# A fused gated-recurrence and SwiGLU kernel: roots by a product for every chunk, gates in turns, decays by products, fills moved, dates shifted by stage

## The chip, the cores and the metric

The kernel runs on one core of a Trainium2 chip. The metric is the device time of one execution in microseconds. A core has a matrix engine (PE, with its weight loads shown as PEld), a vector engine (DVE), an engine for functions of one operand (ACT), a general engine (POOL), and a queue engine (SP) which here only starts transfers. ACT and POOL can start transfers too. Each engine runs its own list of instructions in order and waits on semaphores.

## The reference

```
# gateloop: batch 4, heads 8, 768 steps, head dimension 48
mag = sqrt(a_re^2 + a_im^2);  scale = min(mag, 0.999) / (mag + 1e-6)
for t in range(768):                       # complex decay for each head and row d
    S_re, S_im = ar*S_re - ai*S_im + k_t v_t^T,  ar*S_im + ai*S_re
    y_t = q_t @ S_re
# feed-forward on x = y as (3072 tokens, 384)
xn  = x / sqrt(mean(x*x) + 1e-6) * rms_g
g   = xn @ w_gate;  val = xn @ w_val       # 384 -> 1536
out = (g * sigmoid(g) * val) @ w_out       # 1536 -> 384
```

All inputs are float32 save the weights, which arrive in 64 bits and are narrowed on the chip.

## The kernel before, in words

The 3072 tokens are cut into 24 chunks of 128 (6 for each batch). A unit is the piece for which gates are worked out: units 0 and 1 hold one chunk each, the other eleven two chunks each. A group is two chunks that go through the feed-forward part together; there are 12.

- `load_gates(u)` and `load_kq(u)` bring a_re, a_im, q and k of a unit, features on the partitions. `gates(u)` has four stages of names: "size" (magnitudes, and a running product of them, with ACT and DVE), "root" (a reciprocal root of that product), "turn" (arctan of the gate, a running sum of angles, sine and cosine), and "rot" (q and k times size and angle, into `rots`). Arctan and sine, and the roots, need different tables on ACT, and a load of a table stands between them. Six transfers for each chunk carry `rots` to `kqs`, heads apart, and six for each unit carry the last column of the sizes, `ends`, to `decays`.
- `attend(n)` takes one chunk: S = k^T q by small products (32 rows each) into banks 4 and 5, a causal mask that DVE copies into `ams`, then y from `ams`, `ves` (the values) and the state of the chunk before, and the new state by way of `kts` and a product with `vns`. Transposes for `kts` use banks 7 and 4. The "norm" stage squares y, sums over features with a product with `ones` into one column of bank 7, writes that as `ssv` (DVE), raises it to -1/2 (POOL, `rss`), and spreads the root over all partitions. For chunks in `SENT`, 4 to 21, two POOL transfers do that, by way of a row of `sqs` to `row`; for the others a product with `ident` writes it into bank 7. DVE multiplies it into `xT`.
- `narrow(i)` brings one of 12 pieces of the weights by POOL's queue into a place that is free in `wo` or `hT`, and ACT and three DVE instructions narrow it. Pieces 0 to 5 are w_gate and w_val in turns (1.5 MB each), 6 to 11 are w_out. POOL keeps at most two under way; piece 3 waits besides for a chunk's kq to land (`CLEAR`).
- `feed(g)` multiplies xT by w_gate and w_val (banks 0 to 3 in turns, ACT takes silu, DVE the product into `hT`), then by w_out; from group 2 on by a scheme with fewer products. 
- `look(i)` reads the weights again to check their range, off the main work.

No instruction is issued where it is written. `add` notes each operation with its engine, an estimated duration and what it reads and writes; `note` derives what it must wait for, from overlapping boxes in a tile. `dates` works back from due times, `schedule` plays all engines forward with those durations and picks on each engine, among the operations that are ready, the one due first, and `issue` then emits everything in that order from one line, L667 of the profile. So one change in an estimate or a due time may reorder every engine. The dictionary `shift` moves the due times of a stage; it is empty here. Where PE would idle in the first 62 us (as planned), `schedule` puts in products of `rots` with itself as fillers, whose result nobody reads.

```
    SENT = range(4, N - 2)
...
        if n in SENT:
            line = sq[0:1, 1]
            dma(line, rss[n % 2], "POOL", slow=SLOW)
            wide = row
            dma(wide, line.unsqueeze(1).to_broadcast([1, P, C]), "POOL", slow=SLOW)
        else:
            wide = ps[:, 0:C]
            mms([(wide, rss[n % 2].to_broadcast([P, P]), ident, True, True)], 0.28)
```

## Time and profile before

| what | value |
|---|---|
| time, median of 3 runs | 730.87 us (729.05 to 731.51) |
| profiled execution, its own time | 727.01 us |
| its span, first to last instruction | 725.3 us |
| mean granted clock of PE | 0.988 |
| first product of the feed-forward part | 57.33 us |
| end of the last product on PE | 719.44 us |
| loads of ACT's table | 67, 1283 ns each |
| decay transfers on SP | 78 |
| root transfers on POOL | 36 |
| fillers on PE | 64 records, two for each product |

A row of the page gives engine, operation, output and inputs, the shapes, the number of records, and then busy time, the mean time of one, and idle time of the engine ahead of it with what ended it. A product in float32 shows as two records. Ends of products are modelled, so rows overlap: what a product costs is read from one start to the next. All operations of the fast path come from one line, so they are told apart by tiles.

### The profile page before, as it was taken

What the parts mean: (1) busy time and instruction counts of PE and PEld (TensorE: products, weight loads), DVE (VectorE), ACT (ScalarE), POOL (GpSimd) and SP (SyncE); (2) the same over time, 40 slices, a digit from 0 to 9 for tenths busy, and PEclk for the clock granted to TensorE, in tenths of its full rate; (3) what the DMA queues carried; (4) which work ended last, traced back from release to release, by engine and by line L of the source; (5) the groups of instructions that cost most, each with busy time, mean ns of one, the idle gap of its engine ahead of it and who ended that gap; (6) DMA issues with size and microseconds to landing.
All of it is one profiled execution on the core that took longest, in us unless ns stands there. A gap on an engine that the chain in (4) does not pass through costs nothing.

```text
span 725.3 us, 16217 instructions
## 1 busy us (share of the span) xinstructions
PE 682.6 (94%) x6870; PEld 596.2 (82%) x6870; DVE 470.0 (65%) x740; ACT 332.3 (46%) x450; POOL 70.4 (10%) x116
## 2 busy tenths in 40 slices
PE   0579999999999999999999999999999999999996
PEld 0468867886889889889889889889889889889885
DVE  5969898888879878879774656658544333134121
ACT  7639858867385864845461633626310110010010
POOL 6123100001100001011011011011011011000000
PEclk9978999999999999999999999999999999999998
DMA  8696665655466464566533333334133132100000
GB/s 296 214 310 190 194 185 156 180 143 128 132 149 155 142 168 119 164 141 170 140 87 76 85 63 63 100 67 91 42 62 61 37 66 34 36 13 2 23 0 27
DMA packets 105728, 81.84 MB, mean 113 GB/s; under 512 B 43664, under 2 KB 96144, under 8 KB 105648
## 3 DMA queue, kind: packets, MB, share of 16 engines
q1 hardware_dynamic: 100432, 64.99, 32.9%
q0 software_dynamic: 4416, 15.35, 9.2%
q8 instruction: 56, 0.92, 0.5%
q10 hardware_dynamic: 800, 0.39, 0.2%
q14 instruction: 24, 0.20, 0.1%
HBM read 55.84 MB, written 4.72 MB: 83 GB/s over the span
## 4 chain that ended last, share of the span: by engine, by line
PE 83%; DVE 5%; DMA 4%; ACT 3%; SPq 2%; issue 1%; POOL 0%; DVEq 0%; ACTq 0%
PE bank L667 83%; DMA ve<-in_v_dram 2%; SPq L667 2%; ACT turns L667 1%; DVE rot L667 1%; DVE turns L667 1%; DMA wo<-in_w_gate_dram 1%; ACT t L667 1%; ACT L667 1%; DMA kq<-rot 1%; DVE hT L667 1%; DMA in<-in_a_re_dram 1%; DVE in L667 0%; DVE t L667 0%; DVE wo L667 0%
## 5 line engine op out<-in xcount | busy, mean ns | idle before, releaser
L667 PE MATMUL bank<-xT,wg 128*128 128x256 f32 x864 | 200.9, 383 | 0.9 <-DVE xT L667 0.9
L667 PE MATMUL bank<-xT,wv 128*128 128x256 f32 x864 | 201.2, 382 | 0.4 <-DVE xT L667 0.4
L667 PEld LDWEIGHTS bank<-xT,wg 128*128 128x128 f32 x864 | 162.2, 191 | 22.8 <-DVE xT L667 1.1
L667 PEld LDWEIGHTS bank<-xT,wv 128*128 128x128 f32 x864 | 161.3, 190 | 23.5 <-issue 1.6
L667 ACT ACTIVATE sg<-bank 128x512 f32<-128x512 f32 x72 | 43.0, 597 | 169.4 <-PE bank L667 168.8
L667 PE MATMUL bank<-wo,hT 128*128 128x192 f32 (+1 forms) x576 | 117.7, 356 | 0.6 <-DVE hT L667 0.6
L667 DVE TENSOR_TENSOR hT<-bank,sg 128x512 f32<-128x512 f32 x72 | 49.5, 688 | 100.1 <-PE bank L667 88.5
L667 PEld LDWEIGHTS bank<-wo,hT 128*128 128x128 f32 x576 | 95.7, 190 | 12.9 <-DVE hT L667 1.1
L667 ACT ACT_TABLE_LOAD x67 | 86.0, 1283 | 16.1 <-DVE rot L667 7.1
L667 POOL TENSOR_TENSOR rs<-ssv,mhalf 128x1 f32<-128x1 f32 x24 | 25.3, 1054 | 498.6 <-DVE ssv L667 468.2
L667 DVE TENSOR_TENSOR rot<-kin,turns 128x768 f32<-128x768 f32 x48 | 44.1, 952 | 3.8 <-DMA kq<-rot 3.4
L667 PE MATMUL bank<-sums,hT 128*128 128x192 f32 x240 | 44.2, 327 | 0.0
L667 ACT ACTIVATE kt<-bank 128x384 f32<-128x384 f32 x40 | 19.2, 486 | 51.9 <-PE bank L667 32.3
L667 ACT ACTIVATE turns<-in 128x768 f32<-128x768 f32 (+1 forms) x39 | 30.1, 791 | 26.5 <-DVE rot L667 14.2
L667 PE MATMUL bank<-am,ve 128*32 128x128 f32 x768 | 39.2, 281 | 0.9 <-DMA ve<-in_v_dram 0.9
L667 PEld LDWEIGHTS bank<-sums,hT 128*128 128x128 f32 x240 | 39.7, 190 | 0.1
L667 PEld LDWEIGHTS bank<-kq 96*32 96x32 f32 x1536 | 30.2, 110 | 10.9 <-issue 7.0
L667 DVE TENSOR_TENSOR hT<-hT 128x768 f32<-128x768 f32 x40 | 38.2, 956 | 0.6
L667 PE MATMUL bank<-kq 96*32 96x128 f32 (+3 forms) x1536 | 35.2, 235 | 3.0 <-DMA kq<-rot 2.9
L667 PE MATMUL bank<-rot 128*128 128x128 f32 x64 | 12.2, 352 | 24.8 <-DVE rot L667 24.8
L667 DVE COPY_PREDICATED am<-causal,bank 128x512 f32<-128x512 int32 x48 | 33.9, 724 | 1.6 <-PE bank L667 1.1
L667 ACT ACTIVATE t<-t 128x768 f32<-128x768 f32 (+1 forms) x39 | 30.9, 792 | 8.7 <-DVE t L667 8.2
(115 smaller groups left out, 741.9 us busy)
## 6 DMA issues: line engine op xcount, KB each, us to landing
kq<-rot SPq DMA_DIRECT2D x144, 128.0 KB, 3.0
kin<-in_q_dram SPq DMA_DIRECT2D x24, 192.0 KB, 3.3
kin<-in_k_dram SPq DMA_DIRECT2D x24, 192.0 KB, 3.4
wo<-in_w_gate_dram SPq DMA_DIRECT2D x6, 768.0 KB, 5.0
out_dram<-ot SPq DMA_DIRECT2D x24, 192.0 KB, 2.2
wo<-in_w_val_dram SPq DMA_DIRECT2D x6, 768.0 KB, 5.7
wo<-in_w_out_dram SPq DMA_DIRECT2D x6, 768.0 KB, 4.3
in<-in_a_re_dram SPq DMA_DIRECT2D x11, 384.0 KB, 6.1
```

The source lines that it names most:

```text
L667: fn(*args, **kw)
```

## The change

Seven things change at once.

- `SENT` is empty: the root of every chunk is spread by a product with `ident`.
- `gates` yields ahead of "turn", and units 0 and 1 run in turns, size and root of both ahead of turn and rot of both; arctan waits for the last two roots.
- `send_decays`: for units 0 and 1, decays come by three small products of `ends` with selection matrices (built by DVE at the start in `ots`) and a copy, in place of six transfers each.
- Fills: most go from POOL to DVE with early due times, am1 to ACT; the causal mask takes 5 selections in place of 8.
- Operations of one `group` (the v transfers of a chunk, the kq transfers of a unit) don't wait for one another.
- DVE and ACT are `patient`: the plan may leave them idle for up to 1.5 us for an operation that is due much earlier. Piece 3 of the weights waits for the kq of chunk 1 in place of chunk 0.
- `shift` gets a table of 58 entries by stage.

```diff
--- before.py
+++ after.py
@@ -470,6 +470,7 @@
     LAND = 2.0
     LANES = 8
     turn = 0.0
+    patient = ("ACT", "DVE")
     BEGIN = {"SP": 0.8, "ACT": 0.8, "POOL": 0.8}
     TABLES = {"silu": ("S",), "sin": ("S", "T"), "arctan": ("T",), "rsqrt": ("A",)}
 
@@ -512,16 +513,16 @@
         for x in self.seen.get(name, ()):
             o, w, q0, q1, l, h = x
             over = q0 < p1 and p0 < q1 and l < hi and lo < h
-            if over and (write or w) and o != op["i"]:
+            if over and (write or w) and o != op["i"] and (not op["group"] or self.ops[o]["group"] != op["group"]):
                 op["deps"].add(o)
-            if not (write and p0 <= q0 and q1 <= p1 and lo <= l and h <= hi):
+            if op["group"] or not (write and p0 <= q0 and q1 <= p1 and lo <= l and h <= hi):
                 kept.append(x)
         kept.append((op["i"], write, p0, p1, lo, hi))
         self.seen[name] = kept
 
-    def add(self, eng, calls, dur, reads=(), writes=(), table=None, land=None, due=None, after=(), behind=(), late=None, mode=None):
+    def add(self, eng, calls, dur, reads=(), writes=(), table=None, land=None, due=None, after=(), behind=(), late=None, mode=None, group=None):
         op = dict(i=len(self.ops), eng=eng, calls=calls, dur=dur, deps=set(), table=table, land=land,
-                  base=due, late=late, mode=mode, stage=self.stage, behind={o["i"] for o in behind})
+                  base=due, late=late, mode=mode, group=group, stage=self.stage, behind={o["i"] for o in behind})
         self.ops.append(op)
         op["deps"].update(o["i"] for o in after)
         for ap in reads:
@@ -624,6 +625,14 @@
                 if pick is None or key < pick[0]:
                     pick = (key, o)
             o = pick[1]
+            if eng in self.patient:
+                for x in waiting[eng]:
+                    if t < ready[x["i"]] < t + o["dur"] - 0.2 and x["due"] < o["due"] - 50.0 and ready[x["i"]] < t + 1.5:
+                        pick = None
+                        free[eng] = max(free[eng], min(ready[y["i"]] for y in waiting[eng] if t < ready[y["i"]]))
+                        break
+                if pick is None:
+                    continue
             waiting[eng].remove(o)
             dur = o["dur"]
             if o["table"] and table not in self.TABLES[o["table"]]:
@@ -633,7 +642,7 @@
             if eng == "PE" and o["mode"] != mode:
                 mode = o["mode"]
                 dur += 0.06
-            if eng == "PE" and self.warm and t < self.warm["until"]:
+            if eng == "PE" and self.warm and t < self.warm["until"] and all("end" in x for x in self.warm["after"]):
                 since = max([free["PE"]] + [x["end"] + self.SYNC for x in self.warm["after"] if not recent])
                 n = int((t - since - 0.3) / 0.43)
                 if n > 0:
@@ -866,21 +875,28 @@
                  (width, -(RE_MAX - RE_MIN) / 2), (mhalf, -0.5), (zeros, 0.0)):
         fill(t, x)
     LATE = 12.0
+    add("POOL", [(make_identity, (nc, ident), {})], 0.5, [], [ident], due=-150.0)
+    fill(causal, 1.0, late=LATE)
+    for x, base in [(causal[:, 0], 0)] + [(causal[b * BLK:(b + 1) * BLK, 1], -BLK * (3 - b)) for b in range(4)]:
+        add("POOL", [(nc.gpsimd.affine_select, (), dict(out=x, in_=x, pattern=[[1, C]], compare_op=ALU.is_ge,
+                                                        fill=0.0, base=base, channel_multiplier=-1))],
+            0.42, [x], [x], late=LATE)
+    for t in banks[4:6]:
+        fill(t, 0.0, eng="DVE", due=-300.0)
+    fill(ams[0], 0.0, eng="DVE", due=-290.0)
+    act(ams[1], zeros[:, 0:C].unsqueeze(1).to_broadcast([P, H, C]), AF.Copy, due=-290.0)
     for t in ves + states:
-        fill(t[:, :, :, D:], 0.0, late=LATE)
-    add("POOL", [(make_identity, (nc, ident), {})], 0.6, [], [ident], late=LATE)
-    fill(causal, 1.0, late=LATE)
-    for e in range(2):
-        for b in range(4):
-            x = causal[b * BLK:(b + 1) * BLK, e]
-            add("POOL", [(nc.gpsimd.affine_select, (), dict(out=x, in_=x, pattern=[[1, C]],
-                                                            compare_op=ALU.is_ge, fill=0.0,
-                                                            base=-BLK * (3 - b if e else b),
-                                                            channel_multiplier=-1))], 0.3, [x], [x], late=LATE)
-    for t in ams:
-        fill(t, 0.0, late=LATE)
-    for t in banks[4:6]:
-        fill(t, 0.0, eng="DVE")
+        fill(t[:, :, :, D:], 0.0, eng="DVE", due=-280.0)
+    pick = ots[0][:, 0:ND * D2].rearrange("p (r x) -> p r x", r=ND)
+    band, head = (ots[1][:, o:o + n] for o, n in ((0, P // H), (16, H)))
+    own = [ots[1][:, o:o + ND * H].rearrange("p (r h) -> p r h", r=ND) for o in (32, 64)]
+    fill(pick, 0.0, eng="DVE", late=LATE)
+    for o, order in ((band, "p (x h) -> p x h"), (head, "p (x h) -> p h x")):
+        add("DVE", [(nc.vector.tensor_reduce, (), dict(out=o, in_=ident.rearrange(order, h=H), axis=mybir.AxisListType.X,
+                                                       op=ALU.add))], 0.3, [ident], [o], late=LATE)
+    for r in range(ND):
+        o = pick[:, r].rearrange("p (x j) -> p x j", j=2 * ND)[:, :, r::ND]
+        copy(o, band.unsqueeze(2).to_broadcast([P, P // H, 2]), late=LATE)
     dma(gcol, rms_g.rearrange("(c p) -> p c", p=P))
 
 
@@ -902,7 +918,7 @@
     AHEAD = 2
     landed = {}
 
-    CLEAR = {3: 0}
+    CLEAR = {3: 1}
 
     def fetch(i, piece, raw, eng):
         to, ap, c, f = piece
@@ -963,12 +979,13 @@
     EARLY = {0: -100.0, 1: -98.0}
     SUMMED = ()
     LIGHT = (0, 1, 2)
-    SENT = range(4, N - 2)
+    SENT = ()
     SLOW = 2.0
     turn = {}
     moved = {}
     HOLD = 1
     begun = []
+    roots = []
     started = []
     cleared = {}
     loaded = {}
@@ -996,7 +1013,8 @@
         t["kq"], t["k"], t["q"] = x, x[:, :, 0], x[:, :, 1]
         for name, ap in (("re", a_re), ("im", a_im)):
             x = dma(t[name], ap[b].rearrange("(h j l) s -> l h j s", j=ND, l=L)[:, :, :, c * C:c * C + T],
-                    "ACT" if u < 2 and name == "im" else "SP", behind=moved[HOLD] if u > 1 else ())
+                    "ACT" if u < 2 and name == "im" else "SP", behind=moved[HOLD] if u > 1 else (),
+                    due=u - 310.0 if u < 2 else None)
             if u < 2 and x["eng"] == "SP":
                 rows_.append(x)
         if u == GATE:
@@ -1009,8 +1027,19 @@
             for i, n in enumerate(UNITS[u]):
                 dma(t[name][:, :, i * C:(i + 1) * C],
                     ap[n].rearrange("d (h t) -> (d h) t", t=C).rearrange("(j p) t -> p j t", p=P),
-                    behind=moved[HOLD] if u > 1 else rows_)
+                    behind=moved[HOLD] if u > 1 else rows_, group=("kq", u))
         return t
+
+    def send_decays(u):
+        ns = UNITS[u]
+        if u < 2:
+            tt(own[u], ends[:, :, u:u + 1].to_broadcast([P, ND, H]), head.unsqueeze(1).to_broadcast([P, ND, H]))
+            ps = banks[u][0:D2, 0:H]
+            mms([(ps, pick[:, r], own[u][:, r], r == 0, r == ND - 1) for r in range(ND)], 0.5)
+            copy(decays[u][:, :, 0], ps)
+            return
+        for r in range(2 * ND):
+            dma(decays[way_of(u)][r:D2:2 * ND], ends[:, r % ND, ns[0]:ns[0] + len(ns)], behind=moved[max(ns[0], 1)])
 
     def gates(u):
         ns = UNITS[u]
@@ -1060,8 +1089,10 @@
         stt(t2, t1, 1.5, t2, ALU.add)
         tt(q, q, t4)
 
+        roots.append(root)
+        yield
         flow.stage = "turn", u
-        act(im, im, AF.Arctan, after=[root])
+        act(im, im, AF.Arctan, after=roots[-2:])
         last = turn.get(u - 1) if ns[0] % NCH else None
         for j in range(ND):
             scan(t3[:, j], im[:, j], zeros[:, 0:T], last[:, j] if last is not None else 0.0,
@@ -1090,8 +1121,7 @@
             moved[n_] = [dma(kqs[n_ % 2][r:D2:2 * ND], rots[n_ % 2][:, r], "SP") for r in range(2 * ND)]
             if n_ < 2:
                 cleared[n_] = copy(seen, kqs[n_ % 2][:, 0, 0:1], eng="POOL")
-        for r in range(2 * ND):
-            dma(decays[way_of(u)][r:D2:2 * ND], ends[:, r % ND, ns[0]:ns[0] + nt], behind=moved[ns[0]])
+        send_decays(u)
 
 
 
@@ -1107,7 +1137,7 @@
         ve, am, kq = ves[n % 3], ams[n % 2], kqs[n % 2]
         first, last = n % NCH == 0, n % NCH == NCH - 1
         vv = vns[0]
-        later = dict(behind=moved[min(n - 1, HOLD)] if n else ())
+        later = dict(behind=moved[min(n - 1, HOLD)] if n else (), group=("v", n))
         rows = v[n * C:(n + 1) * C, :].rearrange("t (m e d) -> t m e d", e=2, d=D)
         dma(ve[:, :, 0, 0:D], rows[:, :, 0], **later)
         for b in range(4):
@@ -1233,7 +1263,7 @@
         flow.stage = "feed", g
         ns = GROUPS[g]
         T = len(ns) * C
-        base = {1: 3072}.get(g, 0)
+        base = 0
         h = hT[:, base:base + NF * T].rearrange("p (i f t) -> p i f t", i=2, f=NF)
         A = {(i, k): h[:, i, k * HD:(k + 1) * HD] for i in range(2) for k in range(2)}
         S3, S4 = A[1, 0], S2
@@ -1305,14 +1335,15 @@
         loaded[u] = load_gates(u)
     for u in range(2):
         load_kq(u, loaded[u])
-    gates(0)
-    gates(1)
+    firsts = [gates(0), gates(1)]
+    for x in firsts * 2:
+        next(x, None)
     for i in range(len(pieces)):
         narrow(i)
     gated = 2
     for n in range(N):
         while gated < NU and UNITS[gated][0] <= n:
-            gates(gated)
+            list(gates(gated))
             gated += 1
         xT = attend(n)
         if n == GROUPS[group_of[n]][-1]:
@@ -1347,6 +1378,20 @@
     filler = rots[0][:, 0]
     flow.warm = dict(after=started, until=WARM, call=[
         (nc.tensor.matmul, (banks[3][:, 0:C],), dict(lhsT=filler[:, 0:C], rhs=filler[:, C:2 * C], start=True, stop=True))])
+    flow.shift = {
+        ("attend", 2): -18.4, ("attend", 4): -7.2, ("attend", 5): -4.6, ("attend", 8): 2.6, ("attend", 12): -2.9,
...
+    }
     flow.schedule()
     with tc.manual_schedule():
         flow.issue()
```

## The prediction

> **What bounds the kernel now.** I read the page's first parts, then busy time by stage, then PE's timeline at the edges of the stages.

> ```profile
> span 725.3 us, 16217 instructions
> PE 682.6 (94%) x6870; PEld 596.2 (82%) x6870; DVE 470.0 (65%) x740; ACT 332.3 (46%) x450; POOL 70.4 (10%) x116
> ...
> PE bank L667 83%; DMA ve<-in_v_dram 2%; SPq L667 2%; ACT turns L667 1%; DVE rot L667 1%; DVE turns L667 1%; DMA wo<-in_w_gate_dram 1%; ACT t L667 1%; ACT L667 1%; DMA kq<-rot 1%; DVE hT L667 1%; DMA in<-in_a_re_dram 1%; DVE in L667 0%; DVE
> ```

> PE is busy for 94% and holds 83% of the chain. The stages (busy time of PE, PEld, DVE, ACT, POOL, then the granted clock) say where the rest is:

> ```profile
> 0.00:24.80 24.80, 0.00 (x0) 0.00 (x0) 17.39 (x32) 20.84 (x34) 11.92 (x36) 1.00 0.82 279
> 24.80:46.96 22.16, 15.56 (x283) 13.74 (x283) 20.84 (x25) 8.19 (x15) 5.55 (x8) 0.97 0.85 247
> 46.96:57.33 10.37, 9.73 (x86) 8.76 (x87) 5.82 (x7) 6.32 (x10) 2.62 (x2) 0.50 0.95 274
> 57.33:135.00 77.67, 75.54 (x750) 60.93 (x750) 70.97 (x101) 57.44 (x75) 8.05 (x14) 0.99 0.66 191
> 135.00:330.00 195.00, 194.19 (x2021) 165.60 (x2021) 162.55 (x254) 127.45 (x159) 14.59 (x21) 1.00 0.56 144
> 330.00:672.00 342.00, 341.95 (x3505) 306.23 (x3503) 181.65 (x310) 108.10 (x153) 27.65 (x35) 1.00 0.29 67
> 672.00:719.44 47.44, 45.58 (x230) 40.96 (x230) 10.82 (x18) 3.92 (x7) 0.00 (x0) 1.00 0.03 11
> ```

> The first feed product starts at 57.33, the last matmul ends at 719.44, and the last output takes 5.86 us more. In the 662.1 us between, PE idles for 2.13 + 0.81 + 0.05 + 1.86 = 4.9 us only. So there are three handles: when the feed starts, what is added to PE's work, and those 4.9 us. Before the feed, PE runs at half clock (0.50), after gaps in which it waited. The chain there is a queue of small transfers, and at the right its end on PE:

> ```profile
> 30.54 8.23 DMA ve<-in_v_dram
> ...
> 40.28 6.54 DMA ve<-in_v_dram
> 46.82 0.14 issue
> 46.96 4.48 PE bank L667 x64
> ```

> [...]six matmuls of 256 columns take 2.75 us as a row, the first such row at 57.33 takes 3.63; the half clock lasted over 10 us[...]. [...]sq<-rs lands in 2.0 us, decay<-ends in 1.8 to 2.0.[...]

> **The roots (every chunk).** For chunks 4 to 21, norm's root goes out by two POOL transfers (2.0 and 3.9 us to landing) and comes back as a row. Now it is spread by a product, as it already is for six chunks. What such a product costs PE is seen where the next one starts:

> ```profile
> 666.14 1.24 PE L667 MATMUL bank<-hT 128*128 128x192 f32 x6
> 667.22 0.38 PE L667 MATMUL bank<-ident,rs 128*128 128x128 f32 x2
> 667.44 1.14 PE L667 MATMUL bank<-wo,hT 128*128 128x192 f32 x6
> ```

> It is 0.22 us, not the 0.38 of the row. 18 x 0.22 = **4.0 us more**, nothing hides it, since PE is full there. Upper bound 0.31 each (start to start at a worse place, 106.09 to 106.42, is 0.33): 5.6. The DVE multiply reads a bank in place of row: 542 against 547 ns, nothing. Gone are 36 POOL issues (10.8 + 9.6 us busy) and POOL's 39.1 us of waiting for them, all beside PE, so no gain. New is that PE, in order, may wait for the root; and bank 7 stays taken until that multiply, which the next chunk's transposes into it queue behind. The order of the new program leaves 12 records of 192 columns (1.95 us) between the sum and its root for many chunks. The path there is DVE's ssv 0.15 and POOL's pow 1.26: some 0.4 us in hand for signals. If a DVE operation of 0.95 stands ahead of ssv, PE waits. I take 0.4 us in all; bounds 0 and 18 x 0.4 = 7.

> **The start.** Gates of units 0 and 1 go in turns, so one load of ACT's table in this stage goes (1.28 us); but unit 0 now waits for pieces of unit 1. Working along the new order with the durations of the trace (ACT 0.43 to 0.52 for 384 columns, DVE 0.47 for 384 and 0.87 for 768): both roots are done at 13.1, arctan of unit 0 at 14.9 (13.5 before), its sine at 20.2, rot0 at 23.6 (24.8 before). Its six kq issues of 0.64 us end at 26.5 (26.6 before): attend 0 starts at 28.6, as now. The gain is in unit 1: its rot ends at 29.4 (34.4 before). SP no longer carries the first 12 decay issues (6 between the two kq sets, 26.66 to 30.50, and 6 later, some 0.64 us each). After four ve issues the second kq set is issued at 29.1 to 32.9 and lands at 35.0; PE began attend 1 at 41.65. Weight piece 3 waits for that landing (CLEAR 1 for 0), so it doesn't compete with it; it is issued at 35.6 against 29.4 and lands at about 45, with no user before.

> Then DVE is the limit: two weight pieces (4.3 us each), the 1.75 us multiply of unit 2, and the masks of attend 1 end at 44.8 (45.1 before). So 6.6 us of earlier kq shrink to little; but the transfers that held attend 1's y to 46.96 are long done and y starts at 44.9. From y to the feed it was 10.4 us at half clock. At full clock y ends at 46.9; DVE's decay copy, 1.7 + 0.9 + 0.9 us of pieces and unit 2 and ssv end at 51.3, pow at 52.5, the multiply, behind 0.5 + 1.7 us of DVE, at 54.05. **Feed at 54.1: 3.2 us gained**, and 0.9 more as its first row is not half-rate (3.63 - 2.75). At half clock y ends at 48.5, the decay copy waits for PE's three small products until 49.8, and the feed starts at 56.3: 1.0 gained. Of unknown: the six decay products (0.3 us each at most, in PE's idle time) and own/decay copies (4 x 0.15, in the chain above).

> **Fills.** DVE idled from 2.03 to 5.92. It gets am0 (1024 columns, 0.95 at the 485 ns of its 512-column fill), five of 256 and one of 288 (0.3 each), two sums and three copies (0.2 each): 3.7 us, ending at 5.7. Cost 0; if the gate input landed sooner, up to 1. ACT's fill (0.17 + 0.88 = 1.05 us, by its 384-column rate) lies in its wait from 3.0 to 4.81. POOL is left with less.

> **Dates and groups.** No work is added; DVE, ACT and SP change order. In the feeds both engines have room from 330 us on (53% and 32% busy), so only the first stages can matter. The 2.1 us of idle PE up to 135 are waits for kq (0.74, 0.71) and kt (0.67). With decays of units 0 and 1 off SP and unit 2 begun sooner, kq is earlier; DVE, 91% busy there, is late next. I take these 2.1 as gone; bounds: all 4.9 gone, or 3 more.

> **Sum:** -3.2 - 0.9 + 4.0 + 0.4 - 2.1 = -1.8, rounded to **-1.7**. The profiled execution took 727.0 us (span 725.3 and 1.7 around), the median of the runs shown is 730.9, 3.9 above it. 727.0 - 1.7 = 725.3 for an execution like that; on the median, **729.2**.

> **Rivals.**
> - More is gained. The timed runs (729.1 to 731.5) lie up to 4.5 above the profiled one, so some waits are missing from it. The long route by two POOL transfers (landing 1.9 to 5.9 us) is a candidate; against it, only 0.4 us of PE's idle time in the trace hangs on row. If all 4.9 us go and some 1 us of those unseen: -1.7 - 2.8 - 1 = -5.5, 725.4.
> - **Slower:** the roots wait on DVE. 0.4 us each at 18 places is 7.2 in place of 0.4: +5.1, 736. It decides from about 0.2 us each (3.6, with the sum above zero by 1.5). For it: 1.95 us of cover against 1.85 of path; against it: the product waited 0.5 us in all over the six chunks that have it now.
> - The half clock stays, as the fillers between the root of chunk 0 and y are 16 products of 0.22, leaving gaps of about 2 us: feed at 56.3, +1.4, 732.3.
> - Nothing changes because the dates only shuffle work behind PE; then the roots' 4.0 stand against the start alone: about 730.

> **Chances.** A measurement tells apart about 0.3%, 2.2 us. Likeliest case 0.36 (0.09 of it beyond -2.2), more gained 0.30, half clock or mere shuffle 0.14 (0.05 of it slower), roots waiting 0.20. Faster 0.39, same 0.36, slower 0.25. The likeliest case alone spans 727 to 731; the range takes in half of the root waits and the larger gain: 724.5 to 735.5.

> **What would show it.** ident,rs x48 records with 0.22 us to the next start and almost no idle time before them; no sq<-rs or row<-sq on POOL; attend 1's first matmul near 35; feed's first at 54 to 56; clock between 45 and 57 (1.0 or 0.5); idle PE from the feed on below 3 us. It is wrong if feed starts after 57 or before 52, or if idle time before ident,rs sums to over 3 us.

## The result, and the profile after

| | before | after |
|---|---|---|
| median of the timed runs, taken together on one chip | 728.77 us (725.43 to 732.29, 20 runs) | 730.62 us (725.33 to 735.87, 20 runs) |
| profiled execution, own time | 727.01 us | 725.36 us |
| its span | 725.3 us | 723.6 us |
| first product of the feed | 57.33 us | 57.10 us |
| feed's first product to the end of PE's last | 661.5 us | 659.9 us |
| ACT table loads | 67 | 64 |
| POOL busy | 70.4 us | 39.2 us |

The ratio after to before is 1.0026, with an interval of 1.0006 to 1.0046: no gain, more likely a small loss. On another chip it was 1.0041 (1.0019 to 1.0063, e1 below). Yet the profiled execution of after is 1.65 us shorter than that of before. Executions of one kernel differ, and those of after spread more than before's (standard deviation 3.5 against 2.0 us in e1's group), with the longer ones mostly at a lower granted clock (in that group 0.991 in the mean of after's shorter half, 0.984 in its longer half). The profiled executions of after, 725.36 and in e1 721.99 us, lie at the low end. So the page shows one of after's better executions, and what makes the usual one longer has to be looked for.

The head of the page, and its line of the chain:

```profile
span 723.6 us, 16287 instructions
PE 684.7 (95%) x6956; PEld 606.4 (84%) x6956; DVE 476.6 (66%) x756; ACT 329.0 (45%) x448; POOL 39.2 (5%) x70
...
PE 88%; ACT 3%; DVE 3%; DMA 2%; issue 2%; SPq 1%; POOL 0%; ACTq 0%; DVEq 0%; POOLq 0%
```

The `ve` transfers have left the chain; PE holds 88% of it, with 2% of "issue", time in which an engine waited for nothing that the profile shows. Most of that 2% lies in the start; one piece of 1.72 us, at 299.25, is looked at below. Busy time by stage, cut at after's own edges (PE, PEld, DVE, ACT, POOL, granted clock, DMA share, GB/s):

```profile
22.38:44.76 22.38, 18.13 (x307) 17.09 (x307) 21.26 (x21) 10.73 (x16) 6.84 (x6) 1.00 0.75 214
44.76:57.10 12.34, 8.78 (x106) 8.18 (x106) 8.71 (x14) 8.81 (x14) 2.70 (x4) 0.73 1.07 354
57.10:135.00 77.90, 77.08 (x706) 63.12 (x706) 69.98 (x96) 48.27 (x65) 8.38 (x15) 1.00 0.56 158
135.00:330.00 195.00, 193.26 (x2091) 167.26 (x2090) 154.97 (x245) 119.72 (x153) 7.55 (x8) 1.00 0.47 130
330.00:672.00 342.00, 341.67 (x3513) 308.91 (x3512) 191.92 (x321) 118.31 (x161) 7.32 (x12) 1.00 0.28 77
```

The stage from y to the feed takes 12.3 us, 2 more than before, and still loses clock (0.73). From there on PE idles 0.82 + 1.74 + 0.33 + 0.31 = 3.2 us. Before it was 4.3 us and not 4.9: PE's last product ends at 718.84, and the 719.44 given for it above is the end of DVE's last copy.

```profile
717.70 1.14 PE L667 MATMUL bank<-wo,hT 128*128 128x192 f32 x6
```

PE's timeline from y to the feed (start, duration, tile, count, idle time before it and what ended it):

```profile
44.76 0.55 PE L676 MATMUL bank<-ident,kq 96*128 96x96 f32 x4 [1.08 <-DVE am L676]
45.23 0.43 PE L676 MATMUL bank<-am,ve 128*32 128x128 f32 x8
...
46.80 0.40 PE L676 MATMUL bank<-kq,state 96*32 96x128 f32 x8
...
52.67 1.44 PE L676 MATMUL bank<-ones,sq 128*128 128x1 f32 x6 [3.56 <-ACT kt L676]
53.97 2.05 PE L676 MATMUL bank<-rot 128*128 128x128 f32 x8
55.82 0.64 PE L676 MATMUL bank<-ident,rs 128*128 128x128 f32 x2
56.25 1.06 PE L676 MATMUL bank<-rot 128*128 128x128 f32 x4
57.10 2.94 PE L676 MATMUL bank<-xT,wg 128*128 128x256 f32 x12
```

y runs at full clock from 45.2 and ends at 47.1, as forecast. Then the product with `ones` comes 3.56 us late. ACT's and POOL's timelines say why:

```profile
48.69 1.71 ACT L676 ACTIVATE wo<-wo 128x1536 int32<-128x1536 uint32 x1 [2.59 <-POOL junk L676]
50.20 0.56 ACT L676 ACTIVATE sq<-bank 128x384 f32<-128x384 f32 x1
...
52.05 0.95 ACT L676 ACTIVATE kt<-bank 128x384 f32<-128x384 f32 x2
```
```profile
35.36 2.69 POOL L676 COPY seen<-kq 96x1 f32<-96x1 f32 x1 [6.24 <-DMA kq<-rot]
37.99 0.78 POOL L676 DMA_DIRECT2D wo<-in_w_val_dram  x1
...
47.69 0.97 POOL L676 COPY junk<-wo 1x1 int32<-1x1 int32 x1 [5.67 <-DMA wo<-in_w_val_dram]
```

ACT stands in order in front of the narrowing of piece 3, and sq and kt queue behind it. Piece 3 now waits for chunk 1's kq; POOL's one-column copy that sees it took 2.69 us, so the piece was issued at 37.99 and was seen at 47.69.

This differs from execution to execution. In the profile of e1, which is the same kernel, that copy took 0.20 us, piece 3 was issued at 36.00 and seen at 46.28, and the feed began 2.2 us earlier, at 54.88:

```profile
35.47 0.20 POOL L676 COPY seen<-kq 96x1 f32<-96x1 f32 x1 [6.18 <-DMA kq<-rot]
...
54.88 2.91 PE L676 MATMUL bank<-xT,wg 128*128 128x256 f32 x12
```

The other new thing is in the waits of PE between 57 us and the end (us in total, times, longest), and on its timeline:

```profile
PE bank L676 <- issue: 1.7, 1, 1.7
PE bank L676 <- DMA kq<-rot: 0.8, 1, 0.8
PE bank L676 <- DVE hT L676: 0.3, 1, 0.3
PE bank L676 <- DVE xT L676: 0.3, 1, 0.3
```
```profile
295.09 0.84 PE L676 MATMUL bank<-vn,kt 128*32 128x48 f32 x46
...
297.52 1.32 PE L676 MATMUL bank<-kq 96*32 96x32 f32 x64
298.77 0.48 PE L676 MATMUL bank<-xT,wv 128*128 128x256 f32 x1
300.97 2.64 PE L676 MATMUL bank<-xT,wv 128*128 128x256 f32 x11 [1.72 <-issue]
```

PE stops in the middle of a row of equal products, between one record and the next, and waits for nothing that the profile shows. It does so right behind a dense run of small products: 176 matmuls with as many weight loads in 3.7 us. After has three runs as dense as this, the others at 467 and 630, without a wait behind them; from the feed on, before's densest 3.7 us hold 136 matmuls, and its trace has no such wait.

### The profile page after: what moved, and what is told of

It reads as the page before. It is cut to its first block, busy times and chain, and to the rows that moved or that the text cites. A ratio compares the mean times of both kernels' runs of the same rounds, so it can differ in the third digit from the quotient of the medians.

```text
span 723.6 us, 16287 instructions
## 1 busy us (share of the span) xinstructions
PE 684.7 (95%) x6956; PEld 606.4 (84%) x6956; DVE 476.6 (66%) x756; ACT 329.0 (45%) x448; POOL 39.2 (5%) x70
## 4 chain that ended last, share of the span: by engine, by line
PE 88%; ACT 3%; DVE 3%; DMA 2%; issue 2%; SPq 1%; POOL 0%; ACTq 0%; DVEq 0%; POOLq 0%
PE bank L676 88%; DMA kq<-rot 1%; ACT t L676 1%; SPq L676 1%; DMA in<-in_a_im_dram 1%; ACT turns L676 1%; DVE turns L676 1%; DVE wv L676 1%; ACT L676 0%; DVE rot L676 0%; POOL rs L676 0%; ACT wo L676 0%; ACT in L676 0%; DVE am L676 0%; ACTq L676 0%
## 5 line engine op out<-in xcount | busy, mean ns | idle before, releaser
L676 PE MATMUL bank<-xT,wv 128*128 128x256 f32 x864 | 199.1, 381 | 1.7 <-issue 1.7
L676 PE MATMUL bank<-wo,hT 128*128 128x192 f32 (+1 forms) x576 | 121.1, 357 | 0.3 <-DVE hT L676 0.3
L676 POOL TENSOR_TENSOR rs<-ssv,mhalf 128x1 f32<-128x1 f32 x24 | 18.9, 788 | 537.6 <-DVE ssv L676 537.6
L676 PE MATMUL bank<-sums,hT 128*128 128x192 f32 x240 | 44.9, 329 | 0.0
L676 ACT ACTIVATE sq<-bank 128x384 f32<-128x384 f32 x24 | 11.8, 493 | 71.4 <-PE bank L676 48.1
L676 PE MATMUL bank<-am,ve 128*32 128x128 f32 x768 | 37.3, 275 | 0.0
L676 PE MATMUL bank<-kq 96*32 96x96 f32 (+3 forms) x1536 | 34.4, 235 | 1.4 <-DMA kq<-rot 1.3
```

Of the source, the lines that this page charges most:

```text
L676: fn(*args, **kw)
```

## The experiments

Each ratio is to the kernel before on the same chip, with its 95% interval. "Fillers" are the products that the plan puts into PE's gaps; after has 25 ahead of 30 us and 11, 5, 4, 4 and 2 between 36 and 57 us.

### Was it the half clock ahead of the feed? (e1 to e4, one chip)

The first theory was that the half clock between 45 and 57 us (mean 0.73 in after: 0.50 from 50.47 to 57.29), and what follows it, costs the time. e1 is after again. e2 doubles or quadruples the fillers in the first four of those gaps, 32 products more (the expectations say 33); e3 moves ACT's narrowing of piece 3 behind the kt copies; e4 does both.

```diff
-        steps += [(at, self.warm["call"] * n) for at, n in self.fillers]
+        more = [n * k for (_, n), k in zip(self.fillers, (1, 2, 2, 4, 2, 1) + (1,) * 99)]    # e2, e4
+        steps += [(at, self.warm["call"] * n) for (at, _), n in zip(self.fillers, more)]
...
+        cast[0]["order"] = max(op["order"] for op in kt) + 0.25                              # e3, e4
```

> The changed kernel once more, unchanged, beside the others of this group. Theory A (half clock in the start): its time varies by several us between executions and follows the mean granted clock, and a profile of a typical execution shows PE at half rate for some us between 36 and 65 where the first profile showed full rate: some 730 us, profile up to 5 us longer than 725.4, all of it before 70 us. Theory B (PE waits for the roots in the steady part): a typical execution differs from the first profile in idle time of PE ahead of ident,rs, spread over 135 to 660 us. Theory C (the two kernels are alike and the start decides by transfers): the feed's first product lies at different times, 54 to 61, with the landing of weight piece 3.

Measured: 730.71 us, ratio 1.0041 (1.0019 to 1.0063).

> The changed kernel with more filler products in the gaps of PE between 36 and 57 us (11, 5, 4, 4 become 22, 10, 16, 8); nothing else is moved. Theory A: PE stays busy and at full clock, the mean clock is 0.991 or above in most executions, the median is 2 to 4 us below that of the changed kernel. Theory B: no change. Theory C: no change, or up to 1 us slower where fillers stand ahead of a product that is ready.

Measured: 722.02 us, ratio 0.9931 (0.9910 to 0.9953), with a spread (standard deviation) of 0.9 us.

> The changed kernel, with ACT's cast of weight piece 3 moved in ACT's list from ahead of the squares of chunk 1 to behind the copies of that chunk's transposes. In the profile of the changed kernel ACT stood in that cast's wait until 48.69, while y had been ready at 47.1, and the sum on PE waited 3.6 us until 52.67. Theory C: sum at about 50, feed at about 55.3 in place of 57.1, median 1.8 us lower (1 to 3). Theory A: the shorter gap also keeps the clock up, 2 to 4 lower. Theory B: the gain shows in the start and is 1 to 2, but a loss against the kernel before remains.

Measured: 729.95 us, ratio 1.0039 (1.0018 to 1.0061). The product with `ones` did start 2.6 us earlier, at 50.09; then PE waited 3.76 us for POOL's root, and the feed began at 57.12. One wait took the place of the other, since POOL's root, too, came late.

> Both edits: more fillers and the late cast. Theory A with C: 3 to 6 us below the changed kernel, about 726. Theory A alone: as with more fillers. Theory C alone: 1.8 below, less up to 1 for fillers that now stand in the way (16 fillers, 3.5 us, in a gap that is shorter).

Measured: 721.45 us, ratio 0.9921 (0.9894 to 0.9949), the fastest version of this study, ahead of both kernels.

So more fillers bring 8.7 us, moving the narrowing nothing. But the feed of e2 begins at 56.67, between the 57.10 and 54.88 of the two profiles of after: the gain isn't ahead of the feed. In e2 the wait "issue" is gone too:

```profile
PE bank L677 <- DVE xT L677: 1.1, 2, 0.7
PE bank L677 <- DVE hT L677: 0.3, 1, 0.3
```

### What the parts are worth (e5 to e8, another chip)

e5 gives the kernel before more fillers in its own gaps; e6 adds the roots by product for all chunks; e7 is e2 with the roots of chunks 4 to 21 as rows again; e8 is after with more fillers and an empty `shift`.

```diff
-    SENT = range(4, N - 2)
+    SENT = ()                       # e6, on e5
...
-    SENT = ()
+    SENT = range(4, N - 2)          # e7, on e2
...
-    flow.shift = { ... }            # e8
```

> The kernel before with more filler products in the gaps of PE between 30 and 57 us (2, 6, 1, 7, 1, 1 become 6, 12, 2, 14, 2, 3, and 7 and 4 new ones ahead of chunk 1's transposes and y). It asks what the change is worth once neither kernel falls to half clock. Its mean clock was 0.991 in the middle, 6.5 us lost, against 9.1 in the changed kernel. Theory A (clock hides a gain of the change): 3 to 5 us below the kernel before, some 723.5, and the changed kernel with fillers (722.0) stays ahead by 1 to 3. Theory D (the change is worth nothing but clock noise): the same 722.0 within 0.5. Theory E (fillers are worth as much here): 5.5 below, so the change would be level.

Measured: 730.13 us, ratio 1.0021 (1.0001 to 1.0041). The feed begins at 54.27, 3 us earlier than before's, and nothing is gained in the end: in its profile a wait for kq at 98.92 is 2.2 us long, and 6.83 us of half clock follow from 99.96.

> The same as the kernel before with more fillers, and the roots of all chunks by a product (SENT empty): the first part of the change alone, with a steady clock. 18 products at 0.22 are 4.0 us: some 727.5, 4.0 above the one without (3 to 6, as the plan is made anew). If the transfers by POOL were the cause of waits: less than 2 above. If the roots wait on DVE: 6 or more above, with idle time ahead of ident,rs.

Measured: 731.23 us, ratio 1.0024 (1.0009 to 1.0040), which is e5's within the noise, where 4.0 us more were expected. The products do cost PE what was forecast: from the feed's first product to PE's last it is busy for 659.7 us, against 659.5 in e5, of which e5 loses 3.4 to half clock and e6 nothing; without that loss it is 3.6 us more. Waits of PE for rs sum to 1.0 us over all 24 chunks. Why the median doesn't show the price is open, and with it whether the POOL transfers had a cost of their own.

> The changed kernel with more fillers, with the roots of chunks 4 to 21 back on POOL's two transfers: that part of the change undone. 4.0 us of products go: 718 against 722.0. If the dates of the stages were fitted to the short way of the root, waits for row come up instead and the gain is under 2.

Measured: 731.97 us, ratio 1.0043 (1.0026 to 1.0060): 1.1% above e2's ratio, some 8 us, where 4 us less were expected. PE idles 4.3 us between 70 and 135 us and 4.1 from 330 to 672.

> The changed kernel with more fillers and without the table of dates: what the table is worth. PE's order after the feed's start changes between products of 32-row tiles and of whole tiles 122 times in the kernel before and 100 times in the changed one; a pair costs about 0.2 us, so fewer pairs are worth some 2 us. Without the table the count of changes should go back up, and the time should be 2 to 4 us above 722.0, 724 to 726; if the table is worth nothing on the chip, 722 within 1.

Measured: 731.16 us, ratio 1.0026 (1.0004 to 1.0048): 1.0% above e2's ratio, some 7 us. From the feed on PE waits 3.2 us for xT and 2.1 for am. It is also busy for longer, 661.3 us against 655.9 in e2, of which 1.7 are lost to half clock (busy time of PE, PEld, DVE, ACT and POOL, e8 and then e2):

```profile
57.09:724.89 667.80, 661.26 (x6538) 582.58 (x6538) 428.92 (x678) 300.04 (x392) 25.39 (x35) 1.00 0.35 96
```
```profile
56.67:713.61 656.94, 655.89 (x6538) 580.55 (x6538) 427.43 (x676) 289.37 (x384) 24.33 (x35) 1.00 0.36 98
```

So for the same number of products the table of dates saves PE some 3.7 us of its own time in these profiles, beside the waits.

Without either of the two, the dates or the roots by product, the gain of e2 is gone. These runs also move PE's instructions, so their differences aren't those of one cause (see e13 to e17).

### Which gap? (e9 to e12, a third chip)

If a full clock, kept up by the fillers in the gaps, were the cause, no fillers there at all must be worst, and the gap that matters must show.

```diff
-(1, 2, 2, 4, 2, 1)
+(1, 0, 0, 0, 0, 0)     # e9: none between 36 and 57 us
+(1, 2, 2, 1, 1, 1)     # e10: more in the first two gaps only, 16 products more than after
+(1, 1, 1, 4, 2, 1)     # e11: more in the last two only, 16 products more
...
-        if u < 2:              # e12: decays of units 0 and 1 by transfers again, each gap's fillers doubled
+        if False:
```

> The changed kernel without any filler product after chunk 0 (11, 5, 4, 4, 2 become 0; the 25 ahead of chunk 0 stay). Theory A (PE's gaps between 36 and 57 let the clock fall to half, and it stays low into the feed): the opposite of more fillers, so slower than the changed kernel's 730.7, some 733 to 737, with a mean clock below 0.987, and the profile shows half clock at 45 to 65 us. If the fillers gained by something else (they hold the start back until transfers have landed, say): the same as the changed kernel, or faster by up to 1.

Measured: 724.91 us, ratio 0.9953 (0.9941 to 0.9966), although the half clock lasts longest of all and doubles the feed's first row:

```profile
35.00:62.00 27.00, 15.37 (x171) 12.67 (x172) 23.76 (x32) 17.39 (x25) 9.76 (x9) 0.63 0.90 288
```
```profile
56.52 5.49 PE L677 MATMUL bank<-xT,wg 128*128 128x256 f32 x12 [0.91 <-DVE xT L677]
```

> The changed kernel with more fillers only in the first two gaps, 38 to 44 us (11 and 5 become 22 and 10). If the clock falls in these gaps: most of the 8.7 us that all the fillers brought, some 724. If it falls in the gap ahead of the sum of chunk 1 (49 to 52.7): nearly nothing, 729 to 731. If each gap alone is enough to lose it: 729 to 731 in this run and in the next.

Measured: 728.19 us, ratio 0.9997 (0.9979 to 1.0015), with an "issue" wait of 2.5 us.

> The changed kernel with more fillers only in the gaps of chunk 1's norm, 48 to 56 us (4 and 4 become 16 and 8). If the clock falls here: most of the 8.7 us, some 724. If it falls earlier, 38 to 44: it is low already when these start, and they last twice as long at half clock and delay the feed by some 2 us, so level or slower, 730 to 733.

Measured: 726.83 us, ratio 0.9978 (0.9956 to 1.0000), with an "issue" wait of 2.9 us.

> The changed kernel with more fillers (each gap doubled), with the decays of units 0 and 1 sent by twelve transfers on SP again: that part undone. Six issues of 0.64 us stand ahead of chunk 1's kq, so its S starts 1.3 us later at least (the four ve issues move behind), 36.7; DVE is late anyway, so the feed stays at 56.7 and the time at 722 to 723. If kq did set the start: feed and time 1.3 to 4 later, 723.5 to 726.

Measured: 737.45 us, ratio 1.0146 (1.0117 to 1.0176). PE waits 2.4 us for the kq of attend 1 and 4.4 for kt, and the feed begins at 62.55, 5.9 us later than in e2. That isn't shown to be the price of the transfers alone: the plan is another one, in which ACT waits 5.31 us for a later unit's a_re ahead of the squares of chunk 1 (until 51.09). It has an "issue" wait of 2.8 us.

The first theory falls with e9: with no gap filled and the longest half clock, its ratio lies 0.7 to 0.9% below those of after, 5 to 6 us. What e2, e4 and e9 have in common, against after, e1, e3, e10, e11 and e12, is that they have no "issue" wait.

### The place in PE's instruction stream (e13 to e18)

Counting all of PE's records in the trace, weight loads and semaphore instructions included, exactly 6081 precede the wait in after, e1, e3, e10, e11 and e12, whatever work they stand for (the expectations below number the weight loads alone, from zero: 3065). The page of after shows a queue that carries instructions:

```profile
q8 instruction: 56, 0.92, 0.6%
```

56 transfers of 0.92 MB in all are 16 KB each, for 2 x 6956 matmuls and weight loads: 248 for each transfer. In e13 to e17, whose lists are longer, there are 57 or 58. So the new theory was: the wait is PE's own instructions arriving late, and it arises where a dense run of small products ends at the edge of the block that such a transfer brings. That a block is 256 instructions was the author's assumption, which e15 and e17 test (6337 records there, 256 more). To test the theory, products of `ident` with itself are put at the head of PE's list, where PE is idle until 16.6 us. A product is 4 instructions, two weight loads and two matmuls (the row of six such products with `rs` in before has x12 of each).

```diff
+        first = min(op["order"] for op in self.ops if op["eng"] == "PE")
+        steps += [(first - 0.25, self.warm["pad"] * 33)]     # e13; 8 in e14, 39 on e2 in e15, 34 on e9 in e16, 64 in e17
...
+    flow.warm = dict(after=started, until=WARM, pad=[
+        (nc.tensor.matmul, (banks[3][:, 0:C],), dict(lhsT=ident, rhs=ident, start=True, stop=True))], call=[
```

> The changed kernel with 33 extra products of ident with itself put at the head of PE's list, where PE has nothing to do until about 16 us; their result goes to a bank that nobody reads, and nothing else is moved. They shift every later PE instruction by 66 records, as the 33 added fillers of e2 did. Position theory (the stall 'issue' near 299 us hangs on where PE's instruction stream is cut into the blocks that its instruction queue brings in, and together with what follows it costs most of the 8.7 us between the changed kernel and e2): no 'issue' stall after 57 us, and a median of 722 to 725 us. Gap theory (fillers in the gaps between 36 and 57 us make the difference, by keeping the clock up): the first feed product near 57, and a median of 729 to 732 us as for the changed kernel.

Measured: 722.66 us (721.97 to 723.85), ratio 0.9926 (0.9897 to 0.9955). The dense run stands where it stood in after, with no wait behind it:

```profile
297.51 1.32 PE L678 MATMUL bank<-kq 96*32 96x32 f32 x64
298.77 2.86 PE L678 MATMUL bank<-xT,wv 128*128 128x256 f32 x12
```

> The same with 8 products in place of 33: 16 records more, between the changed kernel (stall of 1.3 to 1.7 us) and e10 and e11 (32 records more, stall of 2.5 to 2.9 us). Position theory: the stall stays, at PE's record 3065 or next to it, 1.5 to 3 us in the profile, and the median stays at 728 to 732 us. If products at the head of PE's list bring something in themselves (a warmer start), it falls below 727 here too. Gap theory: 729 to 732 us.

Measured: 727.47 us, ratio 0.9980 (0.9961 to 1.0000). The wait is longer, again with 6081 records ahead, and now inside the small products; half clock follows at once:

```profile
297.98 1.15 PE L678 MATMUL bank<-kq 96*32 96x32 f32 x49
302.64 0.71 PE L678 MATMUL bank<-kq 96*32 96x128 f32 x15 [3.50 <-issue]
```
```profile
302.60:306.20 3.60, 3.56 (x22) 2.82 (x23) 0.89 (x2) 1.22 (x1) 0.00 (x0) 0.53 0.53 126
```

> e2 (more fillers in the gaps, no stall, 722.0 us) with 39 products of ident at the head of PE's list: with its 33 added fillers 72 products, 288 instructions, which is one block of 256 instructions and 8 products more than the changed kernel. Position theory: the stall is back near 297 us, now at PE's record 3193, 1.5 to 3 us in the profile, and the median rises to 726 to 730 us although the gaps stay filled. Gap theory: no such effect, 721 to 724 us.

Measured: 728.51 us, ratio 1.0008 (0.9991 to 1.0025): 39 idle-time products undo all that e2 had gained. The wait is 2.24 us, with 6337 records ahead, 256 more than in after, and half clock follows for 3.41 us.

> e9 (no fillers between 36 and 57 us, no stall, 724.9 us) with 34 products of ident at the head of PE's list: with the 26 that it lacks this is 8 products more than the changed kernel. Position theory: the stall is back near 300 us at PE's record 3065, and the median rises to 728 to 733 us. Gap theory in the form that e9 left (no gap filled is as good as all filled): 724 to 726 us.

Measured: 731.04 us, ratio 1.0019 (0.9995 to 1.0043), with a wait of 2.42 us behind 6081 records; e9's gain is undone as well.

> The changed kernel with 64 products of ident at the head of PE's list: 256 instructions, one whole block of PE's instruction stream by the position theory, so every later instruction stands in its block where the changed kernel has it. Position theory: the stall stays near 297 us, now at PE's record 3193, and the median at 728 to 732 us, though more products are added than in e13. If it is only that enough products at the head move PE on or warm it, the median is 722 to 725 us as in e13.

Measured: 731.55 us, ratio 1.0037 (1.0016 to 1.0058), as slow as after, with nearly twice the products of e13. 6337 records precede the wait:

```profile
302.14 0.48 PE L678 MATMUL bank<-xT,wv 128*128 128x256 f32 x1
304.71 1.65 PE L678 MATMUL bank<-xT,wv 128*128 128x256 f32 x3 [2.08 <-issue]
```

> The kernel before with the 33 products of ident of e13 at the head of PE's list. Its profile has no 'issue' stall after 57 us. Position theory: nothing to gain, a ratio of 0.997 to 1.003 to the kernel before, or slower if the shift makes a stall. If products at the head help any kernel, it gains about 6 us as the changed kernel did.

Measured: 739.93 us, ratio 1.0169 (1.0127 to 1.0210). It doesn't serve as the control it was meant to be: in before PE's first products come at 24.71, and the 33 products ran from 28.25 to 35.8, in front of attend 0 (35.71, against 28.71), not in idle time. Later in the start PE waits 5.47 us for "issue" ahead of attend 1 (51.19). That wait is of another kind: a semaphore instruction of PE's lasts through it and ends at 51.13, and the last transfer of chunk 1's kq lands at 51.10. In the waits of the other runs no semaphore instruction lies. Whether products in idle time change the kernel before is left open.

### What they say together

| kernels | products more than after | gaps filled | "issue" wait, us | ratio |
|---|---|---|---|---|
| after, e1, e3 | 0 | as planned | 1.7, 1.3, 1.1 | 1.0026, 1.0041, 1.0039 |
| e14 | 8 | as planned | 3.5 | 0.9980 |
| e16 | 8 | none | 2.4 | 1.0019 |
| e10, e11 | 16 | half of them | 2.5, 2.9 | 0.9997, 0.9978 |
| e17 | 64 | as planned | 2.1 | 1.0037 |
| e15 | 71 | all | 2.2 | 1.0008 |
| e13 | 33 | as planned | none | 0.9926 |
| e2, e4 | 32 | all | none | 0.9931, 0.9921 |
| e9 | -26 | none | none | 0.9953 |

e12 is left out, since its start is another one; e8, whose plan is another one too, has a short wait of this kind, 0.46 us at 165.5 with 3009 records ahead, 12 x 256 fewer than 6081.

The wait decides, not the gaps: as planned, all or none filled, each was run with the wait and without it, and each is faster without, by 0.5% or more of the ratio (0.9926 against 0.9980, 0.9931 against 1.0008, 0.9953 against 1.0019). The period is 64 products, 256 instructions (e17, e15).

That PE waits for its instructions is seen in the times of the queue q8. Its transfers are counted from zero here. If transfer 22 brings the block that begins behind 6081 records, transfer 23 brings the one behind 6337, and so on in steps of 256. In all 20 traces together, 1078 such blocks, PE never starts a block less than 2.2 us after its transfer began; in the ten waits it starts 2.2 to 2.5 us after, however long the wait. So the wait ends with this transfer, and its length is set by when the transfer begins. In after it begins at 298.71, when PE has 2 records left: 9.2 us and 471 records after the one before it, and 2.9 us after PE had started the last block that it had. PE goes through that block in 3.0 us. Two other blocks of after take it as little (2.8 us), but their successors were under way 1.2 to 1.3 us before they started, and there is no wait. So a dense block and a late transfer come together here. Why the transfer is late there is open.

The size is explained in part. A wait of 2.1 to 3.5 us with a half-clock stretch of 3.41 us behind it (worth 3.41 x 0.5 = 1.7) makes 3.8 to 5.2 us. e17's profiled span is 8.4 us above e13's: 2.1 + 1.7 for this wait, and 2.72 + 1.7 for a wait for kq at 94.62 and the half clock behind it, 8.2 in all (its feed begins 1.8 us sooner than e13's, and as much goes to other waits and half clock):

```profile
94.62 1.33 PE L678 MATMUL bank<-kq 96*32 96x128 f32 x64 [2.72 <-DMA kq<-rot]
```

That second wait was 0.8 in after, 0.7 in e1 and absent in e2, e13 and e14. Why it should go with the first is open.

## Why the prediction was wrong

The forecast was 1.7 us gained, on the median too. The profiled execution gained 1.65; the median lost 1.85. The agreement of the first is luck: some 4 us that were forecast did not come, and some 4 us that were not forecast came.

The step that failed is "No work is added; DVE, ACT and SP change order", with nothing set down for it. PE's own order changed too, and that brought a wait of PE for its instructions, 1.1 to 3.5 us and in most profiles 1.7 us of lost clock behind it, which no term of the sum has. Without this wait the same change gains 5.4 us (e13).

- **Roots.** Right as a price on PE. 24 products are two records each (x48), and the next start is 0.22 us later:

```profile
605.09 0.38 PE L676 MATMUL bank<-ident,rs 128*128 128x128 f32 x2
605.31 0.98 PE L676 MATMUL bank<-sums,hT 128*128 128x192 f32 x5
```

  PE waited for a root once, 2.65 us for chunk 0 in the start, not after 57 us. The slower rival, roots waiting on DVE, did not occur. In e6 the 18 products took 3.6 us of PE's time (4.0 forecast), though e6's median doesn't show them.
- **The start up to y.** Right in size: attend 1 began at 35.35 (35.0 forecast), y at 45.2 at full clock (44.9). Attend 0 came at 30.14, not 28.6, as 25 fillers stood in front of it.
- **From y to the feed.** This step failed in the profiled execution: 54.1 was forecast, 57.10 measured, so of 3.2 us 0.2 came. The term was piece 3 "at about 45, with no user before". It was seen at 47.69, and ACT's narrowing of it stood in line ahead of sq and kt; the path was followed along DVE and not along ACT's queue. e3 shows that POOL would have been late next. In e1's profile, where POOL's copy was short, the feed began at 54.88, so the forecast was near what the kernel can do, and what it missed is how far this stage varies.
- **Dates and groups.** "These 2.1 as gone" holds in the main: 0.82 us are left up to 135. The 4.9 us of idle time were 4.3, as PE's last product had ended 0.6 us before 719.44. The change of PE's own order went both ways. On the good side, PE is busy from the feed on for 656.7 us, 657.3 before, though the roots added 4.0; half clock explains 0.8 of this, so some 3.8 us of PE's time were saved that the forecast doesn't have. e8 agrees: without the table of dates PE's time is 3.7 us longer than in e2. Part of it may be the changes between 32-row and whole-tile products, which fall from 122 to 100 in the traces from the feed on (112 in e8). Six records of wo,hT take 1.08 us to the next start behind such a change (604.01 to 605.09) and six of hT 0.98 without one (606.29 to 607.27), so some 0.1 us each, 2.2 us in all; this is an estimate, and the rest of the 3.8 is open. On the bad side, attend's small products now come in one dense run at the edge of an instruction block, and PE runs dry there. With that wait the ratio is 0.998 to 1.004 in after, e1, e14 and e17, without it 0.9926 (e13).
- **From the profiled execution to the median.** The sum was made against one execution and laid on the median unchanged. This was the second failure: after's profiled execution has 1.7 us of the new wait and full clock behind it, where six of the ten profiles with the wait (1.1 to 3.5 us) have 3.41 us of half clock right behind it or, in e12, 1.3 us later. Without the wait (e13) the change is worth 0.74% (5.4 us of 728.6), more than was forecast.
- **The half clock.** The prediction priced it twice: 0.9 us for the feed's first row, and a feed at 56.3 in place of 54.1 if it stayed on from y. In after y ran at full clock (1.00 from 44.76 to 50.47) and the first row took 2.94 us; that gaps of about 2 us would keep the clock at half up to there was the author's estimate. At its worst, in e9, that row took 5.49 us against 2.75 at full clock, and e9 was still faster than before. So half clock ahead of the feed is a cost, but not what decided the result.

## What to carry to other kernels

Where PE waits for "issue" between two equal products, see first that no semaphore instruction of its own lies in the gap, and then count its instructions up to that place: if it is the same in variants that differ ahead of it, as the 6081 records here were in after, e1, e3 and e10 to e12, the stream of instructions is the first suspect, and products in idle time can move the edge of a block away from the place (33 did in e13; with 8 in e14 and 64 in e17 the wait stayed). A change that reorders a full engine can be judged only after that, since otherwise its gain or loss hangs on where a block happens to end: 33 idle products were worth 7 to 8 us here, more than the whole change is without the wait. And a profile is one execution: where timed runs spread more than before, ask what it doesn't show.
